# Gated attention and two MLP mixers on one core: unpadded gate/q/k rows, a scan kept in PSUM with VectorE forming q, two small operations swapped, two dummy products fewer

## The chip, the core and the metric

The kernel runs on one core of a Trainium2 chip. The metric is the device time in microseconds (us) of one execution. TensorE (PE) multiplies matrices and writes PSUM; VectorE (DVE), ScalarE (ACT) and GpSimd (POOL) work element by element; SyncE's queue (SP) issues all the transfers. [...]

## What is computed

A gated linear attention over 768 steps, for 4 batches of 8 heads of dimension 48, and behind it two MLP mixers:

```
f = 1 / (1 + exp(-f_logit))
for t in range(768):                       # per batch and head; the state is 48 x 48
    state = f[t, :, None] * state + outer(k[t], v[t])
    y[t] = q[t] @ state
u = x + (x.T @ U @ V).T                    # x: the heads of y side by side, 768 x 384
x = u + relu(u @ w_ch1) @ w_ch2            # 384 -> 1536 -> 384
h = gelu(x @ w_in); u, v = halves of h     # 384 -> 1024
out = x + (u * (w_sg @ layernorm(v) + b_sg)) @ w_out
```

## The kernel before

The attention is cut into 6 chunks of 128 steps for each batch. One transfer pair brings a chunk's gate logits, q and k as a tile of 112 rows (two heads of 48, one at row 0 and one at row 64), with 4 head pairs of 128 steps each for f, q and k: 3 x 512 columns and 16 columns of zeros, 1552 in all (`QW`). For chunks 0 and 1 of batch 0 the f, k and q parts are brought by transfers of their own; from chunk 2 on a tile comes in two halves of 776 columns.

For each chunk `a_decay` takes the sigmoid of f on ScalarE, into PSUM (pool "at") for batch 0 and in place in SBUF for later batches. VectorE scans it backwards into g (L333), takes the minimum-limited first decay, `gmin` (L336), the chunk's total decay, `fall` (L338), and the reciprocal (L339), all of 112 x 4 elements; POOL multiplies k by g (L341). `a_grow` scans f forwards (L350) into the f part of the chunk's SBUF tile and multiplies q by it (L352): on VectorE for later batches and for chunks 0 and 1 of batch 0, on POOL for chunks 2 to 5 of batch 0. `a_scores` multiplies k and q on TensorE (L365), masks the scores (L371 on VectorE; for batch 0 one of the two halves goes through ScalarE, L373, and POOL, L374) and transposes k (L379, L381). `a_out` forms the chunk's output (L392, L397) and the state's new part (L411, L415), which ScalarE scales by `fall` into T (L426).

Batch 0's attention stands in an order written out by hand: everything is issued engine by engine as the code says, the preparation of chunk c+2 (`a_scan`) ahead of the scores of chunk c+1 and the output of chunk c. Between its steps the weights of the first mixer are put together from 64-bit inputs: ScalarE (L250), VectorE (L246, L255, L256), ScalarE and POOL (L285, L287). Products of the identity with itself (`warm`, L528) fill TensorE at three places: 7 at the start, 4 behind the scores of chunk 0, 1 at the end of the attention. Then the first mixer's MLP runs for each batch in 24 steps (L80 and L503 on TensorE, L519 on ScalarE, L520 on VectorE); the attention of the next batch lies between the steps by a table of places (`plan`). The second mixer ends the kernel.

The semaphore that tells POOL of VectorE's scan (L333) before L341 is waited for in one of two ways, as the built program has it: L341 waits for it itself, or a separate wait stands ahead of L341. In the trace L341 starts 0.08 us behind the scan's end in the first way and 0.13 to 0.15 us in the second. The first way is that of chunks 3, 4 and 5 of batch 0, chunks 0, 1 and 2 of batch 1, and chunks 2 and 5 of batches 2 and 3.

Of the kernel before, what the change touches and what calls it, by code (L numbers as in the profile page):

```python
# [13 lines left out]
ALU = mybir.AluOpType  # L14
# [5 lines left out]
C = 128  # L20
NCH = S // C
NP = H // 2
# [6 lines left out]
KH = HF // 128  # L29
HT = S // 2  # L30
PR = 112
QW = 1552
GC = 0.7978845608028654
GA = 0.044715
LIMIT = 1e-15
# [16 lines left out]
def kernel(  # L52
# [16 lines left out]
    vec, act, pool, pe = nc.vector, nc.scalar, nc.gpsimd, nc.tensor  # L69
# [4 lines left out]
    gmin = keep.tile([PR, B * NCH, NP], F32, name="gmin")  # L74
# [34 lines left out]
    def flat(t):  # L109
        return t.rearrange("p a b -> p (a b)")  # L110
# [17 lines left out]
    def fast_path():  # L128
        with ExitStack() as st:
            fast(st)  # L130

    def fast(st):
# [7 lines left out]
        def bank(kind, shape):  # L140
            n = {"h": 2, "ch": 3, "at": 3}[kind]
            return ps.tile(shape, F32, tag=kind, bufs=n, name="ps_" + kind)
# [37 lines left out]
        fone = cst.tile([PR, NP, C], F32, name="fone")  # L180
# [14 lines left out]
        def room(b, c):  # L195
            if b == 0 and c > 2:
                x = flat(xT[6 - c])
                t, vv = x[0:PR, 0:QW], x[:, QW:QW + DM]
            else:
                t = ld.tile([PR, QW], F32, tag="fqk", name="fqk")  # L200
                vv = ld.tile([128, DM], F32, tag="v", name="v")
            tiles[b, c] = dict(t=t, v=vv)
            return t, vv

        def load(b, c):
            t, vv = room(b, c)
            for x in range(0, QW, QW // 2):
                nc.sync.dma_start(t[:, x:x + QW // 2], fqk[b, c, :, x:x + QW // 2])
            nc.sync.dma_start(vv, v[b, c * C:(c + 1) * C, :])
# [106 lines left out]
        def a_decay(b, c):  # L316
            e = tiles[b, c]
            t = e["t"]
            n = NP * C
            flat_f = t[:, 0:n]  # L320
            if b:
                f, scanned = flat_f, flat_f
            else:
                scanned = bank("at", [PR, 512])
                f = scanned
            act.activation(f, flat_f, ACTF.Sigmoid)
            f3 = f.rearrange("p (h t) -> p h t", h=NP)
            g = gs[(b * NCH + c) % 3]

            def back(a, first, m):  # L330
                return bass.AP(a.tensor, a.offset + first, [list(a.ap[0]), [-1, m]])

            vec.tensor_tensor_scan(back(g, n - 2, n - 1), back(scanned, n - 1, n - 1), back(gone, n - 2, n - 1), 1.0,  # L333
                                   op0=ALU.mult, op1=ALU.max)
            i = b * NCH + c
            vec.tensor_scalar(gmin[:, i, :, None], g[:, :, 0:1], LIMIT, None, op0=ALU.max)  # L336
            fall = aw.tile([PR, NP, 1], F32, tag="fall", name="fall", bufs=4)
            vec.tensor_tensor(fall, g[:, :, 0:1], f3[:, :, 0:1], op=ALU.mult)  # L338
            vec.reciprocal(fone[:, :, 0:1], gmin[:, i, :, None])  # L339
            k = t[:, 2 * n:3 * n]  # L340
            pool.tensor_tensor(k, k, g.rearrange("p h t -> p (h t)"), op=ALU.mult)  # L341
            e["f"] = f
            e["fall"] = fall
            e["k"] = k.rearrange("p (h t) -> p h t", h=NP)

        def a_grow(b, c):
            e = tiles[b, c]
            n = NP * C
            flat_f, q = e["t"][:, 0:n], e["t"][:, n:2 * n]
            vec.tensor_tensor_scan(flat_f, e["f"], fone.rearrange("p h t -> p (h t)"), 1.0, op0=ALU.mult, op1=ALU.max)  # L350
            eng = vec if b or c < 2 else pool
            eng.tensor_tensor(q, q, flat_f, op=ALU.mult)  # L352
            e["q"] = q.rearrange("p (h t) -> p h t", h=NP)

        def a_scan(b, c):
            a_decay(b, c)
            a_grow(b, c)
# [167 lines left out]
        def warm(n, w=3):  # L525
            t = bank("h", [128, w, 128])
            for _ in range(n):
                pe.matmul(t, lhsT=ident, rhs=ident[:, None, :].to_broadcast([128, w, 128]), start=True, stop=True)  # L528
# [11 lines left out]
        get("v0", "v1", 0, 1, 2)  # L540
        a_scan(0, 1)
        a_scores(0, 0)
        warm(4)
        early = {0: "u", 2: "v0", 3: "v1", 4: 0}
        for c in range(NCH):
            if c + 2 < NCH:
# [376 lines left out]
def _layout(inputs):  # L923
    import numpy as np

    a = {}
    fqk = np.zeros((B, NCH, PR, QW), np.float32)
    fqk[:, :, :, 0:NP * C] = 30.0
# [43 lines left out]
```

## Time and profile before

| | before |
|---|---|
| median of 3 runs | 701.71 us (700.63 to 702.71) |
| profiled execution, time | 701.85 us |
| profiled execution, span of the trace | 700.0 us |
| TensorE busy | 680.6 us, 97% |
| VectorE busy | 436.3 us, 62% |
| ScalarE busy | 265.0 us, 38% |
| GpSimd busy | 241.8 us, 35% |
| mean granted TensorE clock | 0.995 |

Busy shares are means over stages of different kinds: the attention of batch 0 (about 0 to 49 us), the MLP steps of batch 0 while weights are still being put together (to about 87 us), MLP steps with the attention of the next batch between them (to about 360 us), and the rest. Idle time of TensorE is 19.4 us in all, of which 5.0 us lie in the last 20 us. A product of 32-bit operands is recorded as two matmuls.

### The profile page before, as it was taken

The numbers are of one execution on the slowest core, as the hardware profiler recorded it, in microseconds if no ns is written. First come the engines' busy times: TensorE is split into PE (matmuls) and PEld (weight loads), VectorE is DVE, ScalarE is ACT, GpSimd is POOL, SyncE is SP. The second block draws the span as 40 slices with busy tenths as digits, with TensorE's granted clock in tenths as the row PEclk, the third lists the DMA queues.
The fourth block names the chain that finished last, engine by engine and source line by source line (L and its number), as shares of the span: only waits on it lengthen the run. The fifth ranks groups of instructions, "written<-read, shape, count | busy, mean of one in ns | idle before, by whom it ended". The sixth has DMA issues, their size and how long they took to land.

```text
span 700.0 us, 12736 instructions
## 1 busy us (share of the span) xinstructions
PE 680.6 (97%) x5157; PEld 643.1 (92%) x5157; DVE 436.3 (62%) x790; ACT 265.0 (38%) x546; POOL 241.8 (35%) x262
## 2 busy tenths in 40 slices
PE   9887989999999999999999999999999999999997
PEld 5667988999999999999999999899899989999996
DVE  7899996735666545565738841486585476458532
ACT  3775632322332322323233533464435154233410
POOL 5645731212212102312113543565354254435030
PEclk9999999999999999999999999999999999999999
DMA  9995011330111320112004422000010001001001
GB/s 222 304 335 199 1 52 53 104 103 1 52 53 52 102 55 0 53 52 53 1 1 143 129 69 68 23 1 1 0 69 1 1 0 68 1 1 59 9 1 72
DMA packets 21010, 44.90 MB, mean 64 GB/s; under 512 B 2544, under 2 KB 10352, under 8 KB 20944
## 3 DMA queue, kind: packets, MB, share of 16 engines
q1 hardware_dynamic: 20944, 44.01, 21.3%
q8 instruction: 42, 0.69, 0.4%
q14 instruction: 24, 0.20, 0.1%
HBM read 39.28 MB, written 4.72 MB: 63 GB/s over the span
## 4 chain that ended last, share of the span: by engine, by line
PE 84%; DVE 10%; DMA 4%; issue 1%; ACT 1%; SPq 0%; DVEq 0%; ACTq 0%
PE ps_h L80 28%; PE ps_ch L503 19%; PE ps_ch L80 13%; PE ps_at L80 13%; PE ps_at L365 3%; PE ps_at L392 3%; DVE z L256 2%; DVE raw L246 2%; PE ps_at L397 1%; DMA xT<-in_fqk_dram 1%; DMA raw<-in_w_v_dram 1%; DVE ps_at L255 1%; PE ps_at L379 1%; PE ps_at L466 1%; DVE z L255 1%; DVE al L520 1%
## 5 line engine op out<-in xcount | busy, mean ns | idle before, releaser
L80 PE MATMUL ps_h<-uh,w 128*128 128x384 f32 x576 | 122.0, 346 | 1.6 <-ACT uh L145 0.9
L520 DVE SCALAR_TENSOR_TENSOR al<-ps_h,ah 128x384 fp32r<-128x384 f32 x96 | 53.3, 555 | 110.6 <-ACT ah L519 110.2
L503 PE MATMUL ps_ch<-ah,w 128*128 128x384 f32 x576 | 115.5, 335 | 0.0
L80 PEld LDWEIGHTS ps_h<-uh,w 128*128 128x128 f32 x576 | 99.9, 190 | 4.2 <-ACT uh L145 1.7
L503 PEld LDWEIGHTS ps_ch<-ah,w 128*128 128x128 f32 x576 | 101.2, 188 | 0.2 <-ACT ah L519 0.2
L519 ACT ACTIVATE ah<-ps_h 128x384 fp32r<-128x384 f32 x96 | 47.0, 490 | 122.7 <-PE ps_h L80 121.7
L341 POOL TENSOR_TENSOR fqk<-fqk,g 112x512 f32<-112x512 f32 x21 | 27.2, 1294 | 149.1 <-DVE g L333 117.3
L503 PE MATMUL ps_ch<-al,w 128*128 128x384 f32 x288 | 65.9, 336 | 2.1 <-DVE al L520 2.0
L80 PE MATMUL ps_h<-ul,w 128*128 128x384 f32 x288 | 65.5, 335 | 0.0
L146 POOL TENSOR_TENSOR ul<-xT,uh 128x384 fp32r<-128x384 f32 x45 | 46.8, 1068 | 47.5 <-ACT uh L145 46.6
L146 POOL TENSOR_TENSOR gtl<-t,gth 128x384 fp32r<-128x384 f32 x32 | 32.7, 1024 | 73.6 <-ACT gth L145 73.6
L503 PEld LDWEIGHTS ps_ch<-al,w 128*128 128x128 f32 x288 | 51.1, 188 | 2.8 <-DVE al L520 2.7
L80 PEld LDWEIGHTS ps_h<-ul,w 128*128 128x128 f32 x288 | 51.8, 189 | 0.0
L145 ACT ACTIVATE gth<-t 128x384 fp32r<-128x384 f32 x32 | 16.8, 526 | 78.0 <-DVE t L749 78.0
L371 DVE TENSOR_TENSOR am<-ps_at,mask 128x512 f32<-128x512 f32 x42 | 27.2, 685 | 19.4 <-PE ps_at L365 19.2
L146 POOL TENSOR_TENSOR vnl<-t,vnh 128x512 fp32r<-128x512 f32 x24 | 31.0, 1293 | 17.8 <-ACT vnh L145 17.8
L146 POOL TENSOR_TENSOR xl<-x,xh 128x384 fp32r<-128x384 f32 x18 | 18.2, 1010 | 54.2 <-ACT xh L145 52.4
L80 PE MATMUL ps_ch<-w,vnh 128*128 128x384 f32 x144 | 36.7, 335 | 0.0
L80 PE MATMUL ps_at<-w,vnh 128*128 128x384 f32 x144 | 36.6, 335 | 0.0
L287 POOL TENSOR_TENSOR w<-z,w 128x384 fp32r<-128x384 f32 x24 | 24.8, 1056 | 20.0 <-ACT w L285 20.0
L365 PEld LDWEIGHTS ps_at<-fqk 48*128 48x128 f32 x336 | 21.5, 188 | 8.1 <-issue 7.6
L126 DVE TENSOR_SCALAR t<-t,mv,rs 128x512 f32<-128x512 f32 x24 | 20.8, 866 | 12.3 <-POOL rs L125 12.3
(219 smaller groups left out, 1493.4 us busy)
## 6 DMA issues: line engine op xcount, KB each, us to landing
fqk<-in_fqk_dram SPq DMA_DIRECT2D x38, 339.5 KB, 4.4
raw<-in_w_dram SPq DMA_DIRECT2D x24, 384.0 KB, 7.9
out_dram<-xT SPq DMA_DIRECT2D x24, 192.0 KB, 2.0
v<-in_v_dram SPq DMA_DIRECT2D x21, 192.0 KB, 4.7
raw<-in_w_in_dram SPq DMA_DIRECT2D x8, 384.0 KB, 3.2
z<-in_w_sg_dram SPq DMA_DIRECT2D x12, 192.0 KB, 2.4
xT<-in_fqk_dram SPq DMA_DIRECT2D x6, 339.5 KB, 9.8
raw<-in_w_out_dram SPq DMA_DIRECT2D x4, 384.0 KB, 3.1
```

Source lines behind the costliest of these rows:

```text
L80: pe.matmul(ps, lhsT=l, rhs=r, start=(i == 0), stop=(i == n - 1))
L126: vec.tensor_scalar(dst, src, mv[:, 0:1], rs, op0=ALU.subtract, op1=ALU.mult)
L145: act.activation(hi, src, ACTF.Copy)
L146: eng.tensor_tensor(lo, src, hi.bitcast(F32), op=ALU.subtract)
L287: pool.tensor_tensor(t[:, 1], s, t[:, 0].bitcast(F32), op=ALU.subtract)
L341: pool.tensor_tensor(k, k, g.rearrange("p h t -> p (h t)"), op=ALU.mult)
L365: pe.matmul(sc[j][:, p, :], lhsT=e["k"][rows, p, :], rhs=e["q"][rows, p, :], start=True, stop=True)
L371: vec.tensor_tensor(am, sc[j], m3, op=ALU.mult)
L392: pe.matmul(y[t, h * D:(h + 1) * D], lhsT=e["am"][h % 2][:, h // 2, t], rhs=vv[:, h * D:(h + 1) * D], start=(h == 0), stop=(c == 0 and h = ...
L503: pe.matmul(ch[d], lhsT=w, rhs=a[i // 2], start=(f == 0 and i == 0), stop=(last and i == 2))
L519: act.activation(ah, hp, ACTF.Relu)
L520: vec.scalar_tensor_tensor(al, hp, 0.0, ah.bitcast(F32), op0=ALU.max, op1=ALU.subtract)
```

## The change

`QW` becomes 1536: the rows of the input array and of the tiles lose the 16 columns of zeros, and the halves become 768 columns. `fall` is computed ahead of `gmin`. The forward scan writes over the sigmoid, where that lies: PSUM in batch 0, the same SBUF place as before in later batches. VectorE multiplies q by it for all chunks; POOL no longer does for any. `warm(4)` becomes `warm(2)`. One line goes, so behind it each line number is one lower.

```diff
-QW = 1552
+QW = 3 * NP * C
@@ a_decay
-            vec.tensor_scalar(gmin[:, i, :, None], g[:, :, 0:1], LIMIT, None, op0=ALU.max)
             fall = aw.tile([PR, NP, 1], F32, tag="fall", name="fall", bufs=4)
             vec.tensor_tensor(fall, g[:, :, 0:1], f3[:, :, 0:1], op=ALU.mult)
+            vec.tensor_scalar(gmin[:, i, :, None], g[:, :, 0:1], LIMIT, None, op0=ALU.max)
@@ a_grow
-            flat_f, q = e["t"][:, 0:n], e["t"][:, n:2 * n]
-            vec.tensor_tensor_scan(flat_f, e["f"], fone.rearrange("p h t -> p (h t)"), 1.0, op0=ALU.mult, op1=ALU.max)
-            eng = vec if b or c < 2 else pool
-            eng.tensor_tensor(q, q, flat_f, op=ALU.mult)
+            f, q = e["f"], e["t"][:, n:2 * n]
+            vec.tensor_tensor_scan(f, f, fone.rearrange("p h t -> p (h t)"), 1.0, op0=ALU.mult, op1=ALU.max)
+            vec.tensor_tensor(q, q, f, op=ALU.mult)
@@ batch 0, behind a_scores(0, 0)
-        warm(4)
+        warm(2)
```

On VectorE, in the preparation of chunk 3 of batch 0 (`ps_at` is the PSUM tile with the sigmoid, `xT_75` the chunk's tile in SBUF, `g_107` the backward scan; a scan is printed here as SCALAR_TENSOR_TENSOR):

```order
 L333 SCALAR_TENSOR_TENSOR g_107<-ps_at,gone 112x511
-L336 TENSOR_SCALAR gmin<-g_107 112x4
-L338 TENSOR_TENSOR fall<-g_107,ps_at 112x4
-L339 RECIPROCAL fone<-gmin 112x4
-L350 SCALAR_TENSOR_TENSOR xT_75<-ps_at,fone 112x512
+L337 TENSOR_TENSOR fall<-g_107,ps_at 112x4
+L338 TENSOR_SCALAR gmin<-g_107 112x4
+L339 RECIPROCAL fone<-gmin 112x4
+L350 SCALAR_TENSOR_TENSOR ps_at<-ps_at,fone 112x512
+L351 TENSOR_TENSOR xT_75<-xT_75,ps_at 112x512
 L309 TENSOR_TENSOR us<-z,us 128x6x32
```

The two small operations have changed places, the scan's output is the PSUM tile, and the product for q stands behind the scan.

On POOL, from chunk 2 to chunk 4 of batch 0:

```order
-L374 TENSOR_TENSOR am<-am,mask 128x512
-L341 TENSOR_TENSOR fqk<-fqk,g_109 112x512
-L352 TENSOR_TENSOR fqk<-fqk 112x512
-L374 TENSOR_TENSOR am<-am,mask 128x512
+L373 TENSOR_TENSOR am<-am,mask 128x512
+L341 TENSOR_TENSOR fqk<-fqk,g_109 112x512
+L373 TENSOR_TENSOR am<-am,mask 128x512
 L341 TENSOR_TENSOR xT_75<-xT_75,g_107 112x512
-L352 TENSOR_TENSOR xT_75<-xT_75 112x512
-L374 TENSOR_TENSOR am<-am,mask 128x512
+L373 TENSOR_TENSOR am<-am,mask 128x512
 L341 TENSOR_TENSOR xT_74<-xT_74,g_108 112x512
```

The products for q are gone, and the masked scores follow the k product directly.

## Rows read from the trace of the kernel before

**Rows 1.** Busy us by stretch: PE, PEld, DVE, ACT, POOL; clock, DMA share, GB/s.
```profile
28.00:40.00 12.00, 10.95 (x192) 8.36 (x190) 10.97 (x16) 8.22 (x23) 7.22 (x6) 1.00 1.05 304
...
87.00:108.00 21.00, 18.48 (x160) 16.86 (x159) 20.02 (x32) 6.09 (x13) 6.72 (x6) 0.96 0.16 44
...
170.00:265.00 95.00, 94.89 (x893) 90.53 (x892) 53.70 (x96) 29.26 (x59) 18.92 (x17) 1.00 0.21 58
```

**Rows 2.** Timeline, VectorE and POOL, chunk 3 of batch 0: start, us, engine, line, operation.
```profile
20.49 0.17 DVE L336 TENSOR_SCALAR gmin<-g 112x4 f32<-112x4 f32 x1
20.54 1.27 POOL L341 TENSOR_TENSOR xT<-xT,g 112x512 f32<-112x512 f32 x1 [2.31 <-DVE g L333]
20.57 0.15 DVE L338 TENSOR_TENSOR fall<-g,ps_at 112x4 f32<-112x4 f32 x1
20.70 0.18 DVE L339 RECIPROCAL fone<-gmin 112x4 f32<-112x4 f32 x1
...
22.21 1.29 POOL L352 TENSOR_TENSOR xT<-xT 112x512 f32<-112x512 f32 x1 [0.41 <-DVE xT L350]
22.30 0.69 DVE L371 TENSOR_TENSOR am<-ps_at,mask 128x512 f32<-128x512 f32 x1
```

**Rows 3.** Timeline, VectorE: chunk 1's q product, and three long waits (in brackets).
```profile
10.78 0.69 DVE L352 TENSOR_TENSOR fqk<-fqk 112x512 f32<-112x512 f32 x1
...
12.70 1.22 DVE L333 TENSOR_TENSOR_SCAN g<-ps_at,gone 112x511 f32<-112x511 f32 x1 [0.62 <-ACT ps_at L326]
...
18.57 0.36 DVE L255 SCALAR_TENSOR_TENSOR z<-z,raw 128x192 int32<-128x192 int32 x1 [1.47 <-ACT z L250]
...
24.13 1.22 DVE L333 TENSOR_TENSOR_SCAN g<-ps_at,gone 112x511 f32<-112x511 f32 x1 [1.14 <-ACT ps_at L326]
```

**Rows 4.** Timeline, VectorE's weight steps beside POOL's products, and later without them.
```profile
27.66 0.98 DVE L246 TENSOR_SCALAR raw<-raw 128x384 int32<-128x384 int32 x1
...
28.35 1.42 POOL L374 TENSOR_TENSOR am<-am,mask 128x512 f32<-128x512 f32 x1
...
28.74 1.44 DVE L255 SCALAR_TENSOR_TENSOR z<-z,raw 128x384 int32<-128x384 int32 x1
...
34.84 0.70 DVE L246 TENSOR_SCALAR raw<-raw 128x384 int32<-128x384 int32 x1
...
40.50 0.55 DVE L255 SCALAR_TENSOR_TENSOR z<-z,raw 128x384 int32<-128x384 int32 x1
...
61.88 0.36 DVE L246 TENSOR_SCALAR raw<-raw 128x384 int32<-128x384 int32 x1
```

**Rows 5.** Timeline, TensorE: the dummy products, the scores behind them, a later wait.
```profile
10.65 2.76 PE L528 MATMUL ps_h<-ident 128*128 128x384 f32 x8
...
13.34 1.16 PE L365 MATMUL ps_at<-fqk 48*128 48x128 f32 x16
...
23.56 1.16 PE L365 MATMUL ps_at<-xT 48*128 48x128 f32 x16 [1.17 <-POOL xT L352]
```

**Rows 6.** Busy time by stretch, transfers: mostly gate/q/k and v, then weights.
```profile
20.00:22.00 2.00, 1.65 (x33) 1.09 (x31) 1.93 (x5) 1.88 (x5) 1.27 (x1) 1.00 1.09 225
28.00:30.00 2.00, 2.00 (x36) 1.51 (x32) 1.90 (x2) 1.51 (x7) 1.77 (x2) 1.00 1.04 391
```

**Rows 7.** Timeline, VectorE and POOL in batch 1, chunk 0 and chunk 3.
```profile
90.11 1.28 POOL L341 TENSOR_TENSOR fqk<-fqk,g 112x512 f32<-112x512 f32 x1 [1.16 <-DVE g L333]
90.15 1.27 DVE L338 TENSOR_TENSOR fall<-g,fqk 112x4 f32<-112x4 f32 x1
...
112.82 0.16 DVE L338 TENSOR_TENSOR fall<-g,fqk 112x4 f32<-112x4 f32 x1
112.84 1.28 POOL L341 TENSOR_TENSOR fqk<-fqk,g 112x512 f32<-112x512 f32 x1 [7.62 <-issue]
```

**Rows 8.** Timeline, TensorE at the third chunk of batch 1.
```profile
105.60 1.32 PE L365 MATMUL ps_at<-fqk 48*128 48x128 f32 x14 [1.36 <-DVE T L436]
```

**Rows 9.** Busy time by stretch, columns as in rows 1: behind that wait.
```profile
107.00:108.00 1.00, 1.00 (x5) 1.00 (x6) 0.97 (x2) 0.10 (x1) 0.00 (x0) 0.50 0.00 0
```

## The prediction

> **What bounds the kernel now.** I read the table of stretches first, then VectorE's timeline of batch 0, then what POOL does beside it, then the transfers. In batch 0's attention VectorE is busy for 10.97 of 12 us, TensorE for 10.95; while batch 1's attention starts, VectorE for 20.02 of 21 us and TensorE for only 18.48; later TensorE is busy for 94.89 of 95 us [rows 1]. So the time moves only by what the change does to VectorE's queue up to about 108 us; from there on TensorE is full and carries an earlier or later start unchanged to the end. The reader should see in the timeline that VectorE's instructions follow each other, with three longer waits (0.62, 1.47, 1.14 us) [rows 3], and that some take far more than their own time: a shift of weights (L246) 0.98 us against 0.36 later, a merge (L255) 1.44 against 0.55, each until a product of POOL ends (that of 28.35 us ends at 29.77, the merge at 30.18) [rows 4]. VectorE and POOL hold each other up, and which instruction stands beside which is what this change alters.
>
> **q on VectorE.** Four products leave POOL (1.29 us each) and go to VectorE. The nearest row for a product of a PSUM and an SBUF operand is L371, 0.69 us; with the 0.04 us that an instruction starts behind one of its own engine on which it depends (gmin ends at 20.66, the reciprocal starts at 20.70) that is 0.73 us [rows 2]. 4 x 0.73 = +2.92 us on the queue. L371 runs unheld while POOL's product of 22.21 us runs, so I expect the new products unheld too.
>
> **What no longer holds VectorE.** Without POOL's q products its mask products follow the k products at once and are done before the weight steps come: the two shifts at 27.66 and 34.84 us fall from 0.98 and 0.70 to 0.36 us, the merge at 28.74 from 1.44 to 0.55, and a second merge, behind the shift of 34.84, in the same way [rows 4]. 0.62 + 0.34 + 2 x 0.89 = -2.74 us. If they met a mask product after all, all of this would stay.
>
> **Dummies.** 8 recorded matmuls in 2.76 us are four dummy products; two fewer are 1.38 us. The scores of chunk 1 start with their end, 13.34 us, and q of chunk 1 is ready near 11.5 us (10.78 + 0.69), so they start up to 1.3 us earlier [rows 3, 5]. Behind them on TensorE is chunk 0's output and state, behind that on ScalarE the scaling of T, and behind that the operation for which L255 waits 1.47 us. VectorE comes there 0.73 us later (chunk 2's q product), ScalarE 1.3 us earlier: the wait closes, -1.47. The wait of 1.14 us for chunk 4's sigmoid hangs on the same chain, now 0.74 us earlier (1.47 - 0.73): it closes wholly where VectorE arrives late anyway, and otherwise by 0.73 us.
>
> **Transfers.** The DMA engines are full in batch 0's attention (shares of 1.04 to 1.09), but move 225 GB/s while gate/q/k and v pass and 391 GB/s while weights do [rows 6]. The new halves of 768 columns are rows of 3072 bytes, the length of the weights' rows. Between no gain and the weights' rate the pieces could land up to 40% sooner. What that can give is bounded by who waits: chunk 2's sigmoid, whose wait is 0.62 us on VectorE [rows 3], and nobody else whose engine was free. The sigmoid now also needs the PSUM buffer that chunk 1's q product reads until about 11.5 us, so I take 0.3 of the 0.62. The columns are zeros that no operation reads: they cost nothing else.
>
> **The scan into PSUM.** No row has a scan that writes PSUM. The scan that reads PSUM takes 1.22 us; I take the same, with 0 and 0.1 us for each of six as ends.
>
> **gmin behind fall.** This is the term on which the sign hangs. Where POOL's L341 waits for the scan itself it starts 0.08 us behind it, and the second of the two small operations starts 0.03 us later still. In batch 1, `fall` (two SBUF operands) stands there and takes 1.27 us instead of 0.16: it ends with POOL's product. With L341 0.02 us behind instead it takes 0.16 [rows 7]. This happens 7 times in later batches. In batch 0 `fall` reads the sigmoid in PSUM and is not held (0.15 us, chunk 3) [rows 2], nor in chunks 4 and 5, whose L341 starts as early. The change puts `gmin` in this second place: one SBUF operand, SBUF output, a TENSOR_SCALAR. No row shows `gmin` while POOL reads. Two rows bound it. L246, the same operation from SBUF to SBUF, is held [rows 4]; the reciprocal, just as small and from SBUF to SBUF, runs at 0.18 us in the middle of POOL's product [rows 2]. I take the row of the same operation: held. Then `gmin` ends with POOL's product, about 1.27 us instead of 0.17, and the reciprocal and the scan, queued behind it on VectorE, go back by 1.09 us: 3 x 1.09 = +3.27 us in chunks 3, 4 and 5 of batch 0. In batch 1 the hold is only moved from `fall` to `gmin`; as the reciprocal needs `gmin` and no longer starts beside the held one, +0.1 us for each of three chunks, +0.3.
>
> [...]
>
> **Sum of the forecast (A).** 2.92 - 2.74 - 1.47 - 1.14 - 0.3 + 3.27 + 0.3 = +0.8 us. Against the profiled execution (701.85 us: a span of 700.0 and 1.85 around it) that is 702.7; its time lies 0.14 us over the median, so 702.5 us. What gain the shorter POOL queue and the dummies bring, `gmin` takes back.
>
> **Rival B: gmin is not held.** It speaks for it that the operation is over in 0.17 us and that one equally small runs through POOL's product. Then the 3.27 falls away, the 1.14 us closes only by 0.73, and about 0.3 us opens before chunk 5's sigmoid: 2.92 - 2.74 - 1.47 - 0.73 - 0.3 + 0.3 = -2.0 us at the start. In batch 1 the three held `fall` are freed as well, 3 x 1.1 us in the stretch in which VectorE is the bound. [...] Between 1.1 and 4.0, I take 2.5. The other four held `fall` lie where TensorE is full: nothing. -4.5 us: 697.2, from 695.7 to 698.6.
>
> **Rival C: slower; gmin is also held where POOL starts 0.02 us behind it.** [...] +0.8 + 3.0: 705.5 us.
>
> **Rival D: the clock.** In A, TensorE's wait before chunk 3's scores grows from 1.17 us [rows 5] to some 1.6 us, since it ends with q 0.3 us earlier but starts 0.74 us earlier. The wait of 1.36 us at 105.60 was followed by the lower level [rows 8, 9]. If that comes here as well, up to 1.5 us more (704.0); if the one at 105 stays away, 1.5 us less (701.0). This is the spread of A, not a case of its own.
>
> **How the numbers follow.** A has 0.54, B 0.37, C 0.09. The forecast is A, 702.5 us, by itself 700.5 to 704.2. About 0.3%, 2.1 us, is what a measurement of this kernel can tell from no change: the limits are 699.6 and 703.8. All of B but 0.02 is faster; of A 0.06 is slower by the clock and 0.02 faster; C is slower. Faster 0.37, same 0.48, slower 0.15. The range leaves out C, the upper tail of A (0.03) and a fifth of B (0.07): 696.3 to 704.3.
>
> **What would show it.** In the trace after: `gmin` (L338) at about 1.27 us in chunks 3, 4 and 5 of batch 0 and in chunks 0, 1 and 2 of batch 1, `fall` at 0.16 us everywhere; the q product (L351) at 0.69 us; L246 and L255 near 28 and 35 us at 0.36 and 0.55 us; the scores of chunk 1 near 12 us; the rate near 20 us above 300 GB/s; the first MLP product (L80) within 1 us of where it starts now. One 2 us earlier, with `gmin` at 0.17 us everywhere, would say B; one 3 us later, with all six of batch 0's `gmin` held, C. A second scan of more than 1.3 us, or the lower clock before 50 us, would break the sum elsewhere.

## The result, and the profile after

| | before | changed |
|---|---|---|
| median of 12 runs each, taken together | 701.35 us (700.07 to 702.71) | 706.55 us (703.35 to 707.85) |
| ratio, with its 95% interval | | 1.0062 [1.0046, 1.0079] |
| profiled execution, time / span | 701.85 / 700.0 us | 703.57 / 701.7 us |
| VectorE / GpSimd busy | 436.3 / 241.8 us | 440.2 / 236.9 us |
| mean granted TensorE clock | 0.995 | 0.993 |

The change makes the kernel slower, by 4.3 us by the ratio and by 5.2 us by the two medians. 706.55 us lies above the forecast (702.5), above its range (704.3) and above rival C (705.5). The profiled execution is one of the three fastest of its twelve; what the traces can say of the 3 us between it and the median stands further down.

The first thing to look at is the term on which the prediction said that the sign hangs. The timeline of VectorE and POOL of the changed kernel, chunks 3, 4 and 5 of batch 0 (start, us, engine, line, operation), answers [rows 2]:

```profile
19.84 0.16 DVE L337 TENSOR_TENSOR fall<-g,ps_at 112x4 f32<-112x4 f32 x1
19.89 1.27 POOL L341 TENSOR_TENSOR xT<-xT,g 112x512 f32<-112x512 f32 x1 [3.00 <-DVE g L333]
19.92 2.50 DVE L338 TENSOR_SCALAR gmin<-g 112x4 f32<-112x4 f32 x1
21.12 1.28 POOL L373 TENSOR_TENSOR am<-am,mask 128x512 f32<-128x512 f32 x1
22.46 0.18 DVE L339 RECIPROCAL fone<-gmin 112x4 f32<-112x4 f32 x1
...
26.70 1.27 POOL L341 TENSOR_TENSOR xT<-xT,g 112x512 f32<-112x512 f32 x1 [4.31 <-DVE g L333]
26.73 2.49 DVE L338 TENSOR_SCALAR gmin<-g 112x4 f32<-112x4 f32 x1
27.93 1.27 POOL L373 TENSOR_TENSOR am<-am,mask 128x512 f32<-128x512 f32 x1
...
35.57 1.28 POOL L341 TENSOR_TENSOR xT<-xT,g 112x512 f32<-112x512 f32 x1 [6.38 <-DVE g L333]
35.60 1.30 DVE L338 TENSOR_SCALAR gmin<-g 112x4 f32<-112x4 f32 x1
36.81 1.27 POOL L373 TENSOR_TENSOR am<-am,mask 128x512 f32<-128x512 f32 x1
```

An operation on four elements, 0.17 us before [rows 2], takes 2.50, 2.49 and 1.30 us. It starts 0.03 us behind POOL's k product each time. In chunk 5 it ends with that product (36.85), in chunks 3 and 4 only with the next one, the mask product that now follows without a gap (22.40 and 29.20). The reciprocal, the second scan and q stand behind it. In this execution the hold costs 2.33 + 2.32 + 1.13 = 5.8 us of VectorE's queue, where the sum had 3.27.

What the rest of the change does there is as the prediction said. Timeline of VectorE in the changed kernel, the scan into PSUM, q of chunk 3, and the weight steps of [rows 4]:

```profile
22.67 1.23 DVE L350 TENSOR_TENSOR_SCAN ps_at<-ps_at,fone 112x512 f32<-112x512 f32 x1
23.94 0.69 DVE L351 TENSOR_TENSOR xT<-xT,ps_at 112x512 f32<-112x512 f32 x1
...
31.94 0.35 DVE L246 TENSOR_SCALAR raw<-raw 128x384 int32<-128x384 int32 x1
32.40 0.56 DVE L255 SCALAR_TENSOR_TENSOR z<-z,raw 128x384 int32<-128x384 int32 x1
```

Who waits for it: TensorE, ahead of chunk 3's scores, and in the end the first mixer's first product. TensorE's timeline of the changed kernel, and below it the same product of the kernel before (the wait is in brackets):

```profile
24.73 0.46 PE L364 MATMUL ps_at<-xT 48*128 48x128 f32 x2 [2.59 <-issue]
...
53.52 2.57 PE L80 MATMUL ps_h<-uh,w 128*128 128x384 f32 x6 [0.86 <-ACT uh L145]
```

```profile
49.28 1.89 PE L80 MATMUL ps_h<-uh,w 128*128 128x384 f32 x6 [0.85 <-ACT uh L145]
```

The wait of 1.17 us [rows 5] is 2.59 us, and the MLP begins 4.24 us later. The busy table of the changed kernel (PE, PEld, DVE, ACT, POOL; clock, DMA share, GB/s) answers [rows 1, 6] and shows the clock behind that wait:

```profile
20.00:22.00 2.00, 2.00 (x52) 1.62 (x48) 2.00 (x2) 1.35 (x4) 2.00 (x2) 1.00 1.05 239
22.00:24.00 2.00, 0.14 (x7) 0.01 (x2) 1.90 (x4) 1.04 (x4) 0.39 (x1) 1.00 1.04 240
26.00:30.00 4.00, 4.00 (x31) 2.70 (x27) 3.90 (x5) 2.07 (x4) 2.49 (x2) 0.57 1.05 402
...
28.00:40.00 12.00, 10.68 (x180) 8.03 (x180) 10.83 (x16) 7.05 (x19) 3.70 (x3) 0.92 1.05 302
87.00:108.00 21.00, 18.69 (x156) 17.25 (x154) 19.88 (x33) 7.01 (x14) 8.81 (x8) 1.00 0.16 44
```

TensorE works for 0.14 of 2 us at 22 to 24, the granted clock is then 0.57 of its full speed from 26 to 30 us, 0.50 at its lowest, and the rate near 20 us is 239 GB/s, not the 300 that was asked for.

### The profile page after: what moved, and what is told of

It is laid out like the page before. It is cut to its first block, busy times and chain, and to the rows that moved or that the text cites. A ratio compares the mean times of both kernels' runs of the same rounds, so it can differ in the third digit from the quotient of the medians.

```text
span 701.7 us, 12723 instructions
## 1 busy us (share of the span) xinstructions
PE 680.5 (97%) x5153; PEld 643.6 (92%) x5153; DVE 440.2 (63%) x794; ACT 265.4 (38%) x546; POOL 236.9 (34%) x258
## 4 chain that ended last, share of the span: by engine, by line
PE 85%; DVE 12%; issue 1%; DMA 1%; ACT 1%; SPq 0%; DVEq 0%; ACTq 0%
PE ps_h L80 28%; PE ps_ch L502 18%; PE ps_ch L80 13%; PE ps_at L80 13%; PE ps_at L364 3%; PE ps_at L391 3%; DVE z L256 2%; PE ps_at L396 1%; DVE raw L246 1%; DVE ps_at L255 1%; DVE g L333 1%; PE ps_at L378 1%; DVE gmin L338 1%; PE ps_at L465 1%; DVE al L519 1%; PE ps_at L441 1%
## 5 line engine op out<-in xcount | busy, mean ns | idle before, releaser
L146 POOL TENSOR_TENSOR gtl<-t,gth 128x384 fp32r<-128x384 f32 x32 | 32.8, 1026 | 73.5 <-ACT gth L145 73.5
L370 DVE TENSOR_TENSOR am<-ps_at,mask 128x512 f32<-128x512 f32 x42 | 27.3, 685 | 19.3 <-PE ps_at L364 19.2
L287 POOL TENSOR_TENSOR w<-z,w 128x384 fp32r<-128x384 f32 x24 | 24.8, 1050 | 18.5 <-ACT w L285 16.2
L364 PE MATMUL ps_at<-fqk 48*128 48x128 f32 x336 | 26.0, 285 | 4.6 <-DVE T L435 1.6
```

What stands on the lines that cost most here:

```text
L146: eng.tensor_tensor(lo, src, hi.bitcast(F32), op=ALU.subtract)
L287: pool.tensor_tensor(t[:, 1], s, t[:, 0].bitcast(F32), op=ALU.subtract)
L364: pe.matmul(sc[j][:, p, :], lhsT=e["k"][rows, p, :], rhs=e["q"][rows, p, :], start=True, stop=True)
L370: vec.tensor_tensor(am, sc[j], m3, op=ALU.mult)
```

## Experiments

T is the theory that gmin's hold behind POOL is the loss and the rest of the change is about neutral. Rivals: the q products and the PSUM scan on VectorE cost more than they free (R1); the two dummies let the clock fall (R2). Each ratio is to runs of the kernel before on the same chip.

**The old order in the changed kernel.** `gmin` stands ahead of `fall` again:

```diff
+            vec.tensor_scalar(gmin[:, i, :, None], g[:, :, 0:1], LIMIT, None, op0=ALU.max)
             fall = aw.tile([PR, NP, 1], F32, tag="fall", name="fall", bufs=4)
             vec.tensor_tensor(fall, g[:, :, 0:1], f3[:, :, 0:1], op=ALU.mult)
-            vec.tensor_scalar(gmin[:, i, :, None], g[:, :, 0:1], LIMIT, None, op0=ALU.max)
```

> The changed kernel with gmin ahead of fall again, as before the change; all else as changed. T (the loss is gmin's hold behind POOL's products, 2.33 + 2.33 + 1.14 = 5.8 us in chunks 3, 4 and 5 of batch 0, and the lower clock behind it): gmin and fall at 0.15 to 0.17 us in batch 0, the first MLP product 5 to 6 us earlier than in the changed kernel (53.52 us), so near 48 us, no clock below 0.9 before 50 us; in batch 1 fall is held again for 1.27 us in chunks 0 to 2; time 699 to 700.5 us. R1 (the q products and the PSUM scan cost VectorE more than they free): still 704 to 706.5 us, the first MLP product behind 51 us. R2 (two dummy products fewer let the clock fall): the clock near 0.5 to 0.6 between 26 and 30 us again, time 702.5 us or more.

Measured: 700.76 us against 701.58, ratio 0.9991 [0.9971, 1.0011]. Timeline of VectorE and POOL with the old order, chunks 3 and 4:

```profile
19.41 0.17 DVE L336 TENSOR_SCALAR gmin<-g 112x4 f32<-112x4 f32 x1
19.45 1.27 POOL L341 TENSOR_TENSOR xT<-xT,g 112x512 f32<-112x512 f32 x1 [2.66 <-DVE g L333]
...
24.97 0.17 DVE L336 TENSOR_SCALAR gmin<-g 112x4 f32<-112x4 f32 x1
25.02 1.27 POOL L341 TENSOR_TENSOR xT<-xT,g 112x512 f32<-112x512 f32 x1 [3.06 <-DVE g L333]
```

gmin now asks 0.04 us ahead of POOL and takes 0.17 us; the first MLP product starts at 48.06 us, 5.46 earlier, and no clock before 50 us is under 1.00. The time is 0.3 us above T's range. The loss is the exchange of two lines. What is left of the change is within 0.3% of no change: R1 and R2 fall.

**The exchange alone**, in the kernel before.

```diff
-            vec.tensor_scalar(gmin[:, i, :, None], g[:, :, 0:1], LIMIT, None, op0=ALU.max)
             fall = aw.tile([PR, NP, 1], F32, tag="fall", name="fall", bufs=4)
             vec.tensor_tensor(fall, g[:, :, 0:1], f3[:, :, 0:1], op=ALU.mult)
+            vec.tensor_scalar(gmin[:, i, :, None], g[:, :, 0:1], LIMIT, None, op0=ALU.max)
```

> The kernel before with nothing but gmin and fall exchanged. T: gmin is held in chunks 3 and 4 through one product of POOL (about 1.27 us and not 2.5), because POOL's product for q still waits for VectorE's scan and leaves a gap; in chunk 5 likewise; 3 x 1.1 = 3.3 us on VectorE, of which up to 1.1 can lie in the wait of 1.14 us: first MLP product 2 to 3.5 us behind that of the kernel before (49.28 us), time 703.5 to 705 us. R1 and R2: the swap costs nothing by itself, 701 to 702 us.

Measured: 706.69 us, 1.0082 [1.0054, 1.0109]. Timeline of VectorE and POOL, chunks 3, 4 and 5:

```profile
20.80 1.28 POOL L341 TENSOR_TENSOR xT<-xT,g 112x512 f32<-112x512 f32 x1 [1.83 <-DVE g L333]
20.84 1.27 DVE L338 TENSOR_SCALAR gmin<-g 112x4 f32<-112x4 f32 x1
23.66 1.29 POOL L352 TENSOR_TENSOR xT<-xT 112x512 f32<-112x512 f32 x1 [1.58 <-DVE xT L350]
...
25.74 0.47 DVE L338 TENSOR_SCALAR gmin<-g 112x4 f32<-112x4 f32 x1
26.15 1.27 POOL L341 TENSOR_TENSOR xT<-xT,g 112x512 f32<-112x512 f32 x1
...
33.50 1.27 DVE L338 TENSOR_SCALAR gmin<-g 112x4 f32<-112x4 f32 x1
```

The hold lasts for one product, as expected: POOL's q product waits 1.58 us for VectorE and leaves the gap in which gmin gets through. In chunk 4 gmin meets the end of a mask product (24.92 to 26.18 us) and loses 0.31 us. Together 2.5 us; the first MLP product comes 2.60 us later (51.88) and the profiled execution takes 704.8 us, in the expected range. The median does not fit: it is 2 us more than that execution, with a mean clock of 0.990 to 0.991 in the other three runs and 0.998 in the profiled one. No trace shows those three. So the time does not tell a hold of one product from one of two: the exchange alone costs 0.82% [0.54, 1.09] with 2.5 us of holds, the whole change 0.62% [0.46, 0.79] with 5.8. The traces do: against the same kernel with gmin first, the first MLP product is 2.60 us later here and 5.46 in the changed kernel.

**Four dummies again**, in the changed kernel.

```diff
-        warm(2)
+        warm(4)
```

> The changed kernel with four dummy products behind the scores of chunk 0 again. T: gmin still takes 2.5, 2.5 and 1.3 us in chunks 3 to 5 of batch 0, the first MLP product stays within 1 us of 53.52, time 705 to 707 us. R2 (the dummies kept the clock up): no clock below 0.9 between 20 and 50 us, time 701 to 702.5 us. R1: as T in time.

Measured: 705.14 us, 1.0060 [1.0033, 1.0087]; gmin 2.50, 1.26 and 1.30 us, the clock 0.50 from 25 to 31 us, the first MLP product at 54.96 us. The dummies are not the cause, and do not keep the clock. Two things are not as T had them: gmin of chunk 4 is held for one product only, and the first MLP product is nonetheless 1.4 us later than in the changed kernel. Why is shown below, under the dummies in TensorE's waits.

**gmin one element at a time.**

```diff
-            vec.tensor_scalar(gmin[:, i, :, None], g[:, :, 0:1], LIMIT, None, op0=ALU.max)
+            for h in range(NP):
+                vec.tensor_scalar(gmin[:, i, h:h + 1], g[:, h, 0:1], LIMIT, None, op0=ALU.max)
```

> The changed kernel with gmin formed by four operations of one element for each partition in place of one of four elements. [...] O (a tensor_scalar from SBUF to SBUF is held whatever its length): the first of the four that comes behind POOL's start takes about 2.4 us in chunks 3 and 4, time 705 to 707 us.

Measured: 700.73 us, 0.9985 [0.9970, 1.0000]. Timeline of VectorE and POOL, batch 0's chunk 3 and batch 1's chunk 0:

```profile
21.06 1.27 POOL L342 TENSOR_TENSOR xT<-xT,g 112x512 f32<-112x512 f32 x1 [3.40 <-DVE g L333]
21.09 0.33 DVE L339 TENSOR_SCALAR gmin<-g 112x1 f32<-112x1 f32 x4
...
91.15 1.29 POOL L342 TENSOR_TENSOR fqk<-fqk,g 112x512 f32<-112x512 f32 x1 [1.16 <-DVE g L333]
91.19 0.33 DVE L339 TENSOR_SCALAR gmin<-g 112x1 f32<-112x1 f32 x4
```

The same order, the same 0.03 us behind POOL, the same function of the same data, and no hold: all four take 0.33 us. So O falls: it is neither the order by itself nor the operation, but the form, one operation of 112 x 4 (2.50 us in chunk 3 of the changed kernel) or four of 112 x 1 (0.33). Why the form decides is not shown. The number of elements alone does not decide: the reciprocal, 112 x 4 and from SBUF to SBUF like gmin, took 0.18 us beside POOL's product [rows 2]. The time is not lower than with the old order (700.76 us), though batch 1 is freed too (0.33 us in its chunk 0): this execution's start is 1.9 us later (first MLP product at 49.98 us), of which the longer gmin explains 6 x 0.16 us, and the rest was not traced to its source.

**gmin first, and fall on POOL in later batches.** With it nothing of VectorE's is second in batch 1 to 3 either.

```diff
+            vec.tensor_scalar(gmin[:, i, :, None], g[:, :, 0:1], LIMIT, None, op0=ALU.max)
             fall = aw.tile([PR, NP, 1], F32, tag="fall", name="fall", bufs=4)
-            vec.tensor_tensor(fall, g[:, :, 0:1], f3[:, :, 0:1], op=ALU.mult)
-            vec.tensor_scalar(gmin[:, i, :, None], g[:, :, 0:1], LIMIT, None, op0=ALU.max)
+            (pool if b else vec).tensor_tensor(fall, g[:, :, 0:1], f3[:, :, 0:1], op=ALU.mult)
```

> The changed kernel with gmin ahead of fall again in batch 0, and with fall of batches 1 to 3 formed on POOL, ahead of its k product, so that VectorE has no second small operation for POOL to hold. T: the start as with the old order alone (first MLP product near 48 us, 1.2 us earlier than before), and in batch 1 chunks 0 to 2 without a hold of 1.1 us each: from the first scan of batch 1 to the reduction of all gmin some 2.5 to 3 us less than before (281.5 us from 88.42 to 369.96): 697 to 698.5 us, the price that rival B gave. R3 (TensorE waits there for something else, and the freed VectorE brings nothing): 700 to 701 us.

Measured: 698.27 us against 700.47, 0.9962 [0.9944, 0.9980]: faster than both kernels. The first MLP product starts at 48.10 us, and from batch 1's first gmin to the reduction of all gmin it takes 276.94 us, before 279.89. That is 2.95 us in the trace, where rival B had 2.5. About half of it goes with the holds of VectorE and half with the clock: other traces in which the clock does not fall there, but `fall` or `gmin` is held, take 278.4 to 278.9 us (table below).

**Dummies in TensorE's waits**, in the changed kernel, to keep the clock while the holds stay.

```diff
+            if c in (2, 3):
+                warm(7 if c == 2 else 3)
             if c + 1 < NCH:
                 a_scores(0, c + 1)
```

> The changed kernel with seven dummy products in TensorE's wait ahead of the scores of chunk 3 and three ahead of those of chunk 4, where it waits for VectorE's q (2.59 and 1.32 us in the changed kernel). The holds of gmin stay. K (the clock that falls behind these waits makes a part of the loss): the clock stays at 1.00 between 24 and 32 us, and the time falls by 1.5 to 3 us to 703.5 to 705 us, with fewer runs of a mean clock below 0.992. H (the hold alone makes the loss, VectorE sets the pace there and the clock costs nothing): 706 to 707 us, the same as without.

Measured: 706.70 us, 1.0075 [1.0051, 1.0100]. Busy table, columns as above:

```profile
22.00:26.00 4.00, 4.00 (x14) 2.20 (x12) 3.90 (x7) 1.30 (x5) 0.08 (x1) 1.00 1.04 315
26.00:30.00 4.00, 4.00 (x64) 3.13 (x65) 3.86 (x7) 1.87 (x4) 2.54 (x2) 1.00 1.03 395
```

The clock is 1.00 where it was 0.57, the first MLP product starts at 53.80 us (53.52 without), and the time is in H's range. It does not follow that the lower clock costs nothing. Seven dummies took 4.78 us and overfilled the wait: chunk 3's scores started at 26.20 us, without them at 24.73, and what the higher clock gains is lost by that. VectorE's timeline at the scan of chunk 5, in the changed kernel, then in this run, then in the run with early shifts (further down), whose code is the changed kernel's up to there; in that one chunk 4's gmin as well:

```profile
34.27 1.22 DVE L333 TENSOR_TENSOR_SCAN g<-ps_at,gone 112x511 f32<-112x511 f32 x1 [0.73 <-ACT ps_at L326]
```

```profile
33.36 1.22 DVE L333 TENSOR_TENSOR_SCAN g<-ps_at,gone 112x511 f32<-112x511 f32 x1 [1.33 <-ACT ps_at L326]
```

```profile
26.43 1.26 DVE L339 TENSOR_SCALAR gmin<-g 112x4 f32<-112x4 f32 x1
...
34.88 1.22 DVE L334 TENSOR_TENSOR_SCAN g<-ps_at,gone 112x511 f32<-112x511 f32 x1 [2.86 <-ACT ps_at L327]
```

The scan waits for a sigmoid, and ScalarE takes that sigmoid behind the state products of chunk 2 on TensorE. From the start of chunk 3's scores to the end of those products TensorE needs 5.42 us where the clock is 1.00 (the kernel before, the exchange alone, this run), 7.81 in the changed kernel, 8.62 with four dummies again and 9.18 with late gmin, where the clock is lower for 7 us (0.50 from 25 to 31 and from 26 to 32). In these two chunk 4's gmin is held for one product (1.26 us), as POOL's mask product comes with a gap of 0.43 us, and VectorE then waits 2.75 and 3.33 us for the sigmoid. With early shifts the clock is lower as long (0.50 from 24 to 30) and gmin takes 1.26 us as well: the three holds cost 4.6 us instead of 5.8, and the first MLP product is 0.62 us later all the same (54.14), behind a wait of 2.86 us for the sigmoid. At clock 1.00 the sigmoid would be there before VectorE is (an estimate from these rows: the scan could start at 34.27 - 2.39 = 31.9 us, VectorE is free at 33.5; with late gmin at 36.14 - 3.76 = 32.4 against 32.8). By this estimate the lower clock costs VectorE 0.73 us in the profiled execution of the changed kernel and 3.3 with late gmin. It follows the hold in chunk 3: in every run without a hold through two products there the clock is 1.00 up to 45 us. H's claim that the clock costs nothing is not shown, and K is not excluded.

**The other parts alone**, in the kernel before: the PSUM scan with q on VectorE, two dummies fewer, rows without padding.

```diff
-            flat_f, q = e["t"][:, 0:n], e["t"][:, n:2 * n]
...
-            eng.tensor_tensor(q, q, flat_f, op=ALU.mult)
+            f, q = e["f"], e["t"][:, n:2 * n]
+            vec.tensor_tensor_scan(f, f, fone.rearrange("p h t -> p (h t)"), 1.0, op0=ALU.mult, op1=ALU.max)
+            vec.tensor_tensor(q, q, f, op=ALU.mult)
```

> The kernel before with one part alone: the second scan into PSUM for batch 0 and its q products on VectorE; order of gmin and fall, padding and four dummies as before. T: four products of 0.73 us more on VectorE, the held weight steps freed (2.74 us): first MLP product within 1 us of that of before (49.28 us), time 700.5 to 702 us. R1 (VectorE loses by it): 703 us or more.

Measured: 700.23 us, 1.0002 [0.9986, 1.0017], the first MLP product at 48.09 us, 1.19 earlier, a little better than T's range.

```diff
-        warm(4)
+        warm(2)
```

> The kernel before with one part alone: two dummy products fewer behind the scores of chunk 0. By the prediction the scores of chunk 1 start up to 1.3 us earlier (13.34 us before), VectorE's wait of 1.47 us for the weights shortens by up to 1.3 us, and the first MLP product comes 0.5 to 1.3 us earlier: 700 to 701 us. R2: the clock falls below 0.9 somewhere between 14 and 40 us, time 702.5 us or more.

Measured: 701.02 us, 1.0007 [0.9988, 1.0026]; the first MLP product at 48.66 us, 0.62 earlier, no lower clock before 100 us. Here the wait of 1.47 us is 0.54.

```diff
-QW = 1552
+QW = 3 * NP * C
```

> The kernel before with one part alone: rows of 1536 columns in place of 1552. The prediction gave it 0.3 us at VectorE's wait of 0.62 us for the sigmoid of chunk 2, and a rate above 300 GB/s near 20 us (225 before). T: the wait stays between 0.5 and 0.8 us, the rate between 20 and 24 us stays within 10% of before, the time within 0.2% of before. Rival (the padding is the gain): the rate above 300 GB/s, the wait under 0.3 us, 700 us or less.

Measured: 700.21 us, 0.9988 [0.9967, 1.0008]. The rate from 20 to 24 us is 245 GB/s against 231, 6% more: the padding held back little. The wait of 0.62 us is gone in this execution, but only since VectorE comes there later (a product for q took 1.46 us), so the 0.3 us stays unmeasured.

Added up, the four parts give +0.82 + 0.02 + 0.07 - 0.12 = +0.79%, the whole change 0.62% [0.46, 0.79]. The interval of the exchange alone, [0.54, 1.09], is the widest of them.

**Where the profiled pair hides a part of the loss.** The first MLP product is 4.24 us later, the reduction of gmin at the end of the attention only 1.46 us (369.96 and 371.42). The rows of the MLP's first steps tell where it comes back. Timeline of VectorE and POOL with the old order (clock 1.00 there), then with fall on POOL (first MLP product at the same time, the clock lower); the weight shifts L246, POOL's products L287, and `al`, for which TensorE waits 2.04 us in the first:

```profile
52.08 2.30 POOL L287 TENSOR_TENSOR w<-z,w 128x384 fp32r<-128x384 f32 x2 [4.39 <-DMA raw<-in_w_dram]
52.36 2.24 DVE L246 TENSOR_SCALAR raw<-raw 128x384 int32<-128x384 int32 x2
...
54.52 0.54 DVE L519 SCALAR_TENSOR_TENSOR al<-ps_h,ah 128x384 fp32r<-128x384 f32 x1
```

```profile
52.40 0.62 DVE L246 TENSOR_SCALAR raw<-raw 128x384 int32<-128x384 int32 x2
52.65 2.22 POOL L287 TENSOR_TENSOR w<-z,w 128x384 fp32r<-128x384 f32 x2 [4.90 <-ACT w L285]
52.93 0.55 DVE L519 SCALAR_TENSOR_TENSOR al<-ps_h,ah 128x384 fp32r<-128x384 f32 x1
```

It is the same hold once more. At clock 1.00 POOL asks 0.28 us ahead of VectorE and holds two shifts through two products; at the lower clock (0.50 to 0.65 from 48 to 52 us) `ah`, which stands ahead of the copies for POOL in ScalarE's queue, starts 1.05 us later (51.67 us, with the old order 50.62), the copies come later with it, VectorE asks first, and `al` comes 1.6 us earlier. Nine of the traces side by side (times in us; a lower clock is one that falls to 0.50; the last column is where it was lower between 100 and 120 us; a small operation is gmin or fall, whichever is first):

| kernel | first MLP product, clock there | those shifts | to batch 1's first small operation | from there to the reduction of gmin | lower clock |
|---|---|---|---|---|---|
| before | 49.28, 1.00 | 2.24 | 40.79 | 279.89 | 106 to 110 |
| old order | 48.06, 1.00 | 2.24 | 40.76 | 280.07 | 105 to 109 |
| exchange alone | 51.88, 1.00 | 2.24 | 40.81 | 280.28 | 109 to 113 |
| dummies in the waits | 53.80, 1.00 | 2.24 | 40.76 | 280.41 | 110 to 115 |
| rows without padding | 49.12, 1.00 | 2.24 | 40.80 | 278.43 | none |
| q on VectorE | 48.09, lower | 1.45 | 39.97 | 278.37 | none |
| changed | 53.52, lower | 0.62 | 39.15 | 278.75 | none |
| four dummies again | 54.96, lower | 0.63 | 39.17 | 278.89 | none |
| fall on POOL | 48.10, lower | 0.62 | 39.15 | 276.94 | none |

So a lower clock at that product goes with a gain of 0.8 to 1.6 us, and its absence near 107 us, where TensorE works without a pause [rows 9], with another 1.0 to 1.5. It has to come at that product: with rows without padding the clock was lower from 57 to 62 us (0.50 from 58 to 61), behind the held shifts, and the stretch is 40.80. The profiled execution of before had neither gain, that of the changed kernel both: 4.24 - 1.64 - 1.14 = +1.46. The changed kernel with dummies in the waits is the like for like of before: +4.52 us at the first MLP product, +5.01 at the reduction, 707.12 us against 701.85. No trace shows the changed kernel near its median. The nearest ones are those of early shifts (705.28 us) and late gmin (706.57), each with one small edit and a mean clock of 0.990, as most of the slower executions of the changed kernel have it: the clock is lower for 7 us between 23 and 33 us (0.50 for 6), and in late gmin, unlike in the profiled execution, again from 111 to 115 us. That the slower executions are like these is not shown.

To see whether it is the shifts or the clock, they were moved: the shifts of weight block 3 ahead of the merge of block 2, first in the changed kernel, then in the kernel with fall on POOL, there with the shifts of block 1 as well.

```diff
-            shift(i)
+            if i != 3:
+                shift(i)
...
-        use_first(2)
-        use_middle(2)
         load(1, 0)
         load(1, 1)
         get(*range(3, KF1))
+        use_first(2)
+        shift(3)
+        use_middle(2)
         bank_first(3)
```

> The changed kernel with the shifts of weight block 3 ahead of the merge of block 2 and nothing else; gmin's holds stay. In the traces so far the time from the first MLP product to gmin of batch 1's first chunk is 40.8 us where the clock was 1.00 at that product and these shifts were held (2.24 us), and 39.2 us where the clock was at its lower level and they were not (0.62 us). T2: the shifts take 0.62 us and the stretch 39.2 us whatever the clock, the time falls by 0.5 to 1.6 us, to 705 to 706 us. C (it is the clock, not the shifts): 40.8 us wherever the clock stays at 1.00; time 706 to 707 us.

Measured: 705.05 us, 1.0061 [1.0038, 1.0085]. The profiled execution had the lower clock (0.50 to 0.76 from 54 to 58 us) and 39.17 us, which both theories give; the intervals of the time overlap. It decides nothing.

The second kernel has besides, in the merge of block 0:

```diff
-            for d, z, (low, high) in zip(dst, zs, raws[i]):
+            for n, (d, z, (low, high)) in enumerate(zip(dst, zs, raws[i])):
+                if i == 0 and n:
+                    shift(1)
...
-            shift(i)
+            if i != 1:
+                shift(i)
```

> The kernel of gmin first and fall on POOL (698.27 us), and besides, two pairs of shifts taken out of POOL's way: those of weight block 1 between the two halves of the merge of block 0 (near 40 us), those of block 3 ahead of the merge of block 2 (near 49 us). T2 (a pair of shifts that comes 0.3 us behind POOL's start is held through two products, 2.25 us for 0.62): both pairs at 0.62 us, the first MLP product up to 0.6 us earlier (from there ScalarE's part of hs is late next), from the first MLP product to the first scan of batch 1 39.2 us at any clock; 696 to 697.8 us. N (the holds lie beside other waits): 698 to 699 us.

Measured: 698.27 us, 0.9954 [0.9937, 0.9971]: no faster than without, and in N's range. But the trace decides on the shifts: the clock is 1.00 at the first MLP product, the shifts are not held (1.16 us for four, 0.63 for the others), and the stretch is 39.17 us, as T2 has it. The gain was lost ahead of it: the first MLP product started at 49.84 us instead of 48.10, with the clock at 0.50 to 0.66 from 45 to 49 us.

**What decides whether one product or two.** In the changed kernel three more operations like `fall`, in chunk 3 alone, so that gmin asks later:

```diff
+            if b == 0 and c == 3:
+                spare = aw.tile([PR, 3 * NP, 1], F32, tag="spare", name="spare", bufs=1)
+                for s in range(3):
+                    vec.tensor_tensor(spare[:, s * NP:(s + 1) * NP], g[:, :, 0:1], f3[:, :, 0:1], op=ALU.mult)
             vec.tensor_scalar(gmin[:, i, :, None], g[:, :, 0:1], LIMIT, None, op0=ALU.max)
```

> The changed kernel with three more operations like fall, into a spare tile, between fall and gmin in chunk 3 of batch 0 alone, so that gmin asks some 0.25 us later. In the traces so far a waiting operation of VectorE was let in between two products of POOL where the second product's input was ready before VectorE asked (chunk 5 of the changed kernel: ScalarE's copy ended at 35.10, gmin asked at 35.60, held 1.30 us), and was held through both where that input became ready while it waited (chunk 3: copy ended at 20.04, gmin asked at 19.92, held 2.50 us). P (this order decides): gmin of chunk 3 now asks behind the end of the copy and is let in after the k product: about 1.05 us, and the chunk's second scan starts some 1.2 us earlier against its first. Q (something else in chunk 3 holds it, whatever the order): about 2.25 us. Chunks 4 and 5 are left as they were.

Timeline of ScalarE, POOL and VectorE, chunk 3 (L376 is the copy for the mask product L377):

```profile
19.95 0.58 ACT L376 ACTIVATE am<-ps_at 128x512 f32<-128x512 f32 x1
20.37 1.28 POOL L345 TENSOR_TENSOR xT<-xT,g 112x512 f32<-112x512 f32 x1 [2.68 <-DVE g L333]
...
20.61 2.31 DVE L342 TENSOR_SCALAR gmin<-g 112x4 f32<-112x4 f32 x1
...
21.61 1.28 POOL L377 TENSOR_TENSOR am<-am,mask 128x512 f32<-128x512 f32 x1
```

The copy ends at 20.53, gmin asks at 20.61, and is held through both all the same. P falls. (The one run took 706.57 us, beside 700.78 for the kernel before.)

## Why the prediction was wrong, point by point

- **The step that failed** is the size of "gmin behind fall". That gmin would be held, in which six places, and that `fall` would not be (0.16 to 0.17 us), came out: 1.27, 1.27 and 1.26 us in batch 1's chunks 0 to 2, 0.16 in chunks 0 to 2 of batch 0, so no run shows the holds there from which C had its +3.0. But the price of one hold was taken as the rest of one product, 3 x 1.09 = 3.27, and it was 5.8 in the profiled execution. The prediction had said itself that the mask products now follow the k products at once, and had used it for the weight steps; it did not carry it to gmin. The exchange alone, where POOL still pauses, has 1.27 us. A second term was missing beside it: nothing stood in A for VectorE's wait ahead of chunk 5. Where chunk 4's gmin is held for one product only (early shifts: 4.6 us of holds in all) that wait is 2.86 us and the start no earlier. Holds and wait together are 6.5 us in the changed kernel and 7.4 with early shifts.
- **The rest of the start.** q on VectorE +2.92 (0.69 us each, not held) and the weight steps -2.74 (0.98, 1.44, 0.70 and 1.44 us became 0.35, 0.56, 0.35 and 0.56) are as predicted. A shift at 16.10 us, 1.01 us beside POOL's products, became 0.25: -0.76 that the sum had missed. The wait of 1.47 became 0.45, not nothing: the scores of chunk 1 started at 12.71 us and waited 1.21 for the PSUM bank that VectorE's masking (L370) frees, not for the dummies. The 1.14 closed, but 0.73 opened ahead of chunk 5, where the sum had 0.3 in B alone; 0.62 became 0.45. With 5.8 that is 2.92 - 2.74 - 0.76 - 1.02 - 1.14 + 0.73 - 0.17 + 5.8 = +3.6 of the 4.24 us measured; 0.14 of the rest stands ahead of chunk 0's small operations, the other 0.5 in small gaps that were not assigned.
- **Transfers.** 239 GB/s in place of more than 300; with the padding gone by itself 6% more. The bound of "no gain" was the better end.
- **The scan into PSUM**: 1.23 us, as taken.
- **Rival B** was well understood and somewhat too cheap. With the old order the start gains 1.2 us where it had 2.0 (the wait ahead of chunk 4 went from 1.14 to 0.94, not by 0.73, the one ahead of chunk 5 opened by 0.53, not 0.3). Freeing batch 1 brings 2.95 us in the trace. The 2.5 taken for it, between 1.1 and 4.0, was the author's estimate, and no run shows it as such: TensorE is idle there for 21 - 18.48 = 2.5 us [rows 1], and the clock of before, 0.70, 0.50, 0.50 and 0.59 from 106 to 110 us, is 1.00 there in the run with fall on POOL. B was 4.5 us under the kernel before; fall on POOL is 0.38% [0.20, 0.56], 1.4 to 3.9 us.
- **Rival D.** The lower clock came where it was feared (0.57 from 26 to 30 us), behind a wait of 2.59 us instead of some 1.6. The price given, up to 1.5 us, was the author's estimate, and no run shows it as such: VectorE waited 0.73 us for the sigmoid behind it in the profiled execution and 2.75 to 3.33 in three others. At the next place its sign was the other one: there the lower clock went with a gain of 1.6 us. Where the one near 107 us stayed away, the stretch behind was 1.0 to 1.5 us shorter.
- **What would show it**: five of the marks came (fall, q, the weight steps, the PSUM scan, gmin in batch 1). The first MLP product was to be within 1 us and was 4.24 late, more than C's 3; the lower clock before 50 us, named as a thing that would break the sum, did so by 0.73 us in the profiled execution.
- **The range.** It took A's spread from the clock and from nothing else. The unknown in the sign's own term, how long one hold can last, had two ends in the rows, until the first product ends or until POOL next pauses; the second was not taken in. The trace of the kernel before has both: a shift of 0.98 us [rows 4], and two shifts of 2.24 us beside two products (the first row of the table above).

## What to carry to other kernels

In the changed kernel a tensor_scalar of VectorE from SBUF to SBUF, of 112 x 4 elements, that asked 0.03 us behind a GpSimd product paid for GpSimd's next product too, which followed without a gap, in two chunks of three (2.50 and 2.49 us, but 1.30 in chunk 5), so its price is read from GpSimd's queue behind the product and not from the product alone. Closing the gap on GpSimd went with a longer hold: 1.27 us in chunk 3 with the gap (the exchange alone), 2.50 without. Put the short operation that others wait for first behind the instruction that starts GpSimd (gmin took 0.17 us there), give GpSimd the second one (2.95 us less from batch 1 on), or bring it into a form that is not held (four operations of one element: 0.33 us). Look at the clock behind a wait of TensorE that a hold opens: behind that of 2.59 us it was 0.57 for 4 us. And compare executions at several marks, not by their ends: two traces of two kernels differed by 4.24 us at one mark and by 1.46 at a later one.

## What was not expected of the hardware

- **A hold through two products.** In the trace of before `fall` was held to the end of the product beside it (1.27 us [rows 7]). In the changed kernel the hold goes on: at the end of POOL's first instruction POOL's second one ran, and VectorE, which had waited 1.2 us, went on waiting (2.50 us for four elements). Two shifts that take 0.62 us elsewhere took 2.24 beside two products in the run with the old order.
- **When VectorE gets in between** stays open. Where POOL pauses between the two products, by 0.43 us or more, gmin of batch 0 was held for one at most. Where it does not, in eight gmin, of chunk 3 (changed, four dummies, dummies in the waits, late gmin), of chunk 5 (changed, four dummies, late gmin) and of chunk 4 (changed), it was held through both wherever ScalarE's copy for the mask product ended behind the start of the k product (20.04 against 19.89 us in chunk 3), and through one where it ended ahead of it (35.10 against 35.57 in chunk 5). The late gmin asked behind the end of that copy and was held through both, so it is not the order of copy and gmin that decides. The gmin of chunk 4 in the exchange alone speaks against the rest as a rule: there the k product's input came (25.63) behind the start of the running mask product (24.92), and gmin still got in between at 26.18.
- **One element was not held.** The same function took 0.33 us in four operations of 112 x 1 beside a running product, and 1.26 to 2.50 us in one of 112 x 4 that started behind it.
- **A lower clock that gains, and one that costs.** With the clock at 0.50 from 54 to 57 us, just behind the first MLP product (53.52), the stretch to batch 1 took 39.15 us, at 1.00 it took 40.8; with the shifts moved it took 39.17 at 1.00, so the gain is that another engine asks first. Between 23 and 33 us, where the clock fell to 0.50, TensorE's part of the chain to chunk 5 took 7.81 to 9.18 us, at 1.00 it took 5.42.
